# Weight chunks requested from ScalarE's queue, and the PSUM banks of the prologue divided anew

## The chip, the cores and the metric

The kernel runs on one core of one Trainium2 chip. A core has five engines that run beside each other, each through its own instructions in program order: TensorE (PE in the profile; its weight loads are PEld), VectorE (DVE), ScalarE (ACT), GpSimd (POOL) and SyncE (SP), which here does nothing but issue transfers. Sixteen DMA engines move the data. The metric is the device time of one execution in microseconds; less is better.

## The reference

Eight batches of eight heads, 576 positions, head size 64, all in fp32. Two attentions are added: one over queries, keys and values averaged in groups of four positions, its result repeated four times, and one in which each position sees the positions less than four away. The heads are then joined to 512 channels, mixed along the sequence by a product of rank 32, and put through a feed-forward network (FFN) with 2048 hidden channels.

```
q_d, k_d, v_d = means over groups of 4 positions       # 144 positions
out_d    = softmax(q_d k_d^T / 8) v_d
out_up   = repeat(out_d, 4)
scores   = q k^T / 8 where |i - j| < 4, else -1e9
x        = out_up + softmax(scores) v                  # heads joined: (8, 576, 512)
u        = x + (x^T U V)^T                             # U: 576 x 32, V: 32 x 576
y        = u + relu(u w_ch1) w_ch2                     # 512 -> 2048 -> 512
```

## The kernel before

**Precision.** TensorE multiplies the large products in fp32r, a shortened fp32. To keep fp32 accuracy each operand is held as a high and a low half, and each product is made of three: high times high, high times low, low times high. So one FFN step, 128 hidden channels of one tile of positions, is 12 matmuls into the hidden bank (`ffn1`, L944) and 12 into the four accumulators (`ffn2`, L969). The first two batches make four tiles of 288 positions, the other six nine tiles of 384. Between the two products ScalarE makes the high half of the rectified hidden values (hH, L952) and VectorE the low half (hL, L953).

**Weights.** Each of the two weight matrices comes in 16 chunks of 128 x 512 values that lie in memory as eight-byte numbers. A chunk (wr) is transferred raw, 512 KB, into the place that its converted form will take, and `convert` turns it into fp32 and splits it: ScalarE takes the upper 16 bits (half, L349), VectorE shifts them into a PSUM bank as y (L352) and joins them with the middle bits (c, L354), ScalarE makes the high half (W, L360), GpSimd the low half (W, L364). The smaller matrices U and V go the same way. `load_w` requests a chunk on SyncE (L416). The list `done` holds the merge step of each chunk so far, and a request is ordered behind the merge of the fourth chunk before it.

**The prologue.** The four head pairs of batch 0 are worked in the early form (`early_global`, `local_blocks`, `early_mix`, `u_tail`): local scores into PSUM banks 0 and 1 (ps_b), pooled scores (ps_s), softmax, products with the values (ps_a, ps_ba), the mixing with U (ps_hu, L708 and L710) and with V (ps_u, L726), and last the two halves uH and uL of the FFN's input. The windows of the values (vw, L598) have one buffer for all pairs. In batch 0 the mixing of a pair uses banks 0 and 1 too, and the conversions take banks 2 and 3 in turn, until 12 chunks are ordered; from then on a conversion uses the second hidden bank, and the FFN's first 19 steps have the other hidden bank alone. The FFN's accumulators take all four banks 0 to 3 from the first `ffn2` step on. The attention of the later batches runs in another form, much of it on GpSimd, through scratch memory in DRAM, while the FFN goes on.

**The order.** The order of all instructions is worked out by a planner in the kernel's Python code (`Plan`). Each operation has an engine, an assumed duration, a priority, what it depends on, and perhaps an earliest time. `run` steps through assumed time, takes for each engine the ready operation of least priority number, and models transfers with one clock `t_dma` on which they follow each other. The resulting list fixes each engine's program; on the chip each engine works through its own in order and waits only for data and buffers. That a request is ordered behind an earlier merge is the planner's doing and is no wait on the chip.

## Time and profile before

| | us |
|---|---|
| time before, median of 3 runs | 1009.38 (1004.36 to 1010.22) |
| profiled execution, its own time | 1009.23 |
| profiled execution, span | 1007.4 |
| TensorE busy | 974.7 |
| GpSimd busy | 571.5 |
| VectorE busy | 445.1 |
| ScalarE busy | 383.1 |

All profile lines are from that one profiled execution; times in them are microseconds from the start of the span, and mean durations are nanoseconds where a line says so. The names of engines are those given above; SPq is the queue of SyncE, whose DMA-issuing instructions, as those of any engine, do not count as busy time. "L416" is a line of the kernel. "out<-in" names what an instruction writes and reads, "x6" how many were taken together. A bracket at the end of a line gives the time for which the engine stood idle before the instruction, and what ended that wait; "issue" stands where the profile shows nothing that it waited for. PEclk, the granted clock, is the share of TensorE's full clock that it was given.

### The profile page before, as it was taken

Reading aid. Unit: us, or ns where it says so; the run is one execution under the profiler, and the core shown is the slowest. Engines: PE = TensorE matmul, PEld = TensorE weight load, DVE = VectorE, ACT = ScalarE, POOL = GpSimd, SP = SyncE. Lnnn points to the kernel's source line nnn. Section 1 sums busy time; section 2 is a strip of 40 time slices with the busy share of each in tenths; the row PEclk is TensorE's granted clock in tenths of the full one; section 3 lists DMA queues with packets and bytes.
Section 4 is the critical chain, followed back from the end, with each engine's and each line's share of the span. In section 5 each row is a group of like instructions: output and inputs, shape, how many; then the busy total and the mean of one; then the engine's idle time right before and its main releaser. Section 6 shows DMA issues by size and latency. Waiting matters only on the chain.

```text
span 1007.4 us, 24554 instructions
## 1 busy us (share of the span) xinstructions
PE 974.7 (97%) x9668; PEld 952.4 (95%) x9668; DVE 445.1 (44%) x852; ACT 383.1 (38%) x1191; POOL 571.5 (57%) x636
## 2 busy tenths in 40 slices
PE   6879999899999999999999999999999999999998
PEld 4769999898999999999999999999999999999998
DVE  5576855545544544544645445265351222211211
ACT  4676754443444443434545344444321222111110
POOL 6675997967858857857867766676650112300100
PEclk9789999999999999999999999999999999999999
DMA  9578876656546657455656366466330121000000
GB/s 275 160 268 239 211 173 143 156 129 152 138 111 161 161 127 149 129 127 139 158 136 146 80 162 148 98 164 146 82 94 1 21 59 25 32 1 1 32 1 32
DMA packets 221243, 120.06 MB, mean 119 GB/s; under 512 B 174580, under 2 KB 197448, under 8 KB 221128
## 3 DMA queue, kind: packets, MB, share of 16 engines
q1 hardware_dynamic: 221128, 118.50, 46.7%
q8 instruction: 76, 1.25, 0.5%
q14 instruction: 39, 0.32, 0.1%
HBM read 87.59 MB, written 30.86 MB: 118 GB/s over the span
## 4 chain that ended last, share of the span: by engine, by line
PE 80%; POOL 5%; DMA 4%; issue 2%; DVE 1%; ACT 1%; SPq 1%; POOLq 0%; DVEq 0%; ACTq 0%
PE acc L969 36%; PE ps_h L944 36%; PE ps_a L575 2%; PE ps_b L756 2%; PE ps_hu L919 2%; POOL W L364 2%; DMA ul<-up_s 1%; PE ps_t L562 1%; POOL Pt L840 1%; PE ps_b L769 1%; DMA vr<-in_v 1%; DMA wr<-in_W 1%; PE ps_u L726 1%; POOL gh L439 1%; POOL vr L533 0%
## 5 line engine op out<-in xcount | busy, mean ns | idle before, releaser
L969 PE MATMUL acc<-hH,W 128*128 128x384 f32 (+1 forms) x1664 | 443.8, 328 | 0.0
L944 PE MATMUL ps_h<-uH,W 128*128 128x384 f32 (+1 forms) x1376 | 359.1, 323 | 4.3 <-DVE hL L953 3.9
L969 PEld LDWEIGHTS acc<-hH,W 128*128 128x128 f32 x1664 | 297.6, 188 | 1.2
L969 PE MATMUL acc<-hL,W 128*128 128x384 f32 (+1 forms) x832 | 268.8, 323 | 0.0
L840 POOL TENSOR_TENSOR Pt<-vl,ms 128x896 f32<-128x896 f32 (+1 forms) x140 | 239.9, 1793 | 37.8 <-DMA vl<-in_vp 18.9
L944 PEld LDWEIGHTS ps_h<-uH,W 128*128 128x128 f32 x1376 | 245.5, 189 | 5.8 <-DVE hL L953 5.0
L953 DVE SCALAR_TENSOR_TENSOR hL<-ps_h,hH 128x384 fp32r<-128x384 f32 (+1 forms) x208 | 108.9, 524 | 314.9 <-ACT hH L952 314.4
L952 ACT ACTIVATE hH<-ps_h 128x384 fp32r<-128x384 f32 (+1 forms) x208 | 97.2, 467 | 329.7 <-PE ps_h L944 318.7
L944 PE MATMUL ps_h<-uL,W 128*128 128x384 f32 (+1 forms) x688 | 221.1, 321 | 0.5 <-POOL uL L735 0.5
L845 DVE TENSOR_REDUCE acc<-Pt 128x128 f32<-128x1024 f32 (+1 forms) x140 | 152.6, 1107 | 73.0 <-POOL Pt L840 40.7
L969 PEld LDWEIGHTS acc<-hL,W 128*128 128x128 f32 x832 | 156.6, 188 | 0.0
L944 PEld LDWEIGHTS ps_h<-uL,W 128*128 128x128 f32 x688 | 130.2, 189 | 0.8 <-POOL uL L735 0.7
L944 PE MATMUL ps_h<-u,W 128*128 128x384 f32 x432 | 99.6, 339 | 0.0
L834 ACT ACTIVATE Pt<-ul 128x128 f32<-128x128 f32 (+1 forms) x140 | 55.6, 432 | 95.7 <-DVE acc L845 68.6
L735 POOL TENSOR_TENSOR uL<-xT,uH 128x384 fp32r<-128x384 f32 (+2 forms) x52 | 41.1, 813 | 79.5 <-ACT uH L733 79.5
L979 POOL TENSOR_TENSOR o<-uH,uL 128x384 f32<-128x384 f32 (+1 forms) x43 | 39.1, 938 | 71.6 <-DMA out_t<-o 71.5
L944 PEld LDWEIGHTS ps_h<-u,W 128*128 128x128 f32 x432 | 77.4, 187 | 0.0
L911 POOL TENSOR_TENSOR xL<-xL,xH 116x640 fp32r<-116x640 f32 x28 | 43.9, 1567 | 56.9 <-ACT xH L910 56.6
L533 POOL TENSOR_TENSOR vr<-vr 72x256 f32<-72x256 f32 x56 | 41.4, 739 | 45.7 <-DMA vr<-in_v 36.1
L787 ACT ACTIVATE se<-ps_b 96x114 f32<-96x114 f32 x112 | 40.0, 357 | 47.9 <-PE ps_b L762 33.2
L364 POOL TENSOR_TENSOR W<-c,W 128x512 fp32r<-128x512 f32 x32 | 41.3, 1299 | 21.8 <-ACT W L360 21.8
L548 ACT ACTIVATE E<-ps_b,nb 72x144 f32<-72x144 f32 x112 | 40.7, 369 | 0.7
(131 smaller groups left out, 950.8 us busy)
## 6 DMA issues: line engine op xcount, KB each, us to landing
wr<-in_W SPq DMA_DIRECT2D x32, 511.8 KB
vl<-in_vp SPq DMA_DIRECT2D x56, 240.0 KB
vr<-in_v SPq DMA_DIRECT2D x64, 144.0 KB
gT<-in_kT SPq DMA_DIRECT2D x28, 291.0 KB
gq<-in_qT SPq DMA_DIRECT2D x28, 288.0 KB
up_s<-od SPq DMA_DIRECT2D x112, 72.0 KB
ul<-up_s SPq DMA_DIRECT2D x28, 288.0 KB
x_s<-acc SPq DMA_DIRECT2D x28, 288.0 KB
```

The source lines that it names most:

```text
L364: pool_tt(1.0 * n, lambda: nc.gpsimd.tensor_tensor(out=lo_out(), in0=ta()[l0:], in1=hi_out()[l0:].bitcast(F32), op=ALU.subtract), [t, *own ...
L533: pool_tt(256, lambda x=x: nc.gpsimd.tensor_tensor(out=x()[:, :, 0:2, :], in0=x()[:, :, 0:2, :], in1=x()[:, :, 2:4, :], op=ALU.add), [x], ...
L548: act(SD, lambda a=a, hh=hh, nb=nb: nc.scalar.activation(Es[hh]()[:, a, :], pooled_view(ps[hh])[:, a], AF.Exp, bias=nb()[:, a:a + 1], scal ...
L735: pool_tt(n, lambda uH=uH, uL=uL, uf=uf, us=us: nc.gpsimd.tensor_tensor(out=uL.ap(hp, us), in0=uf(), in1=uH.ap(hp, us).bitcast(F32), op=AL ...
L834: act(n * D, lambda n=n, ps=ps, Pt=Pt: nc.scalar.activation(Pt()[:, :n, :, 7], ul()[:, ps, :], AF.Copy), [ul], [(Pt, 1)], prio, 0.16)
L840: nc.gpsimd.tensor_tensor(out=Pt()[:, :n, :, 0:7].rearrange("p s d o -> p o s d"), in0=win, in1=at()[:, ps, :].rearrange("p s o -> p o s") ...
L845: dve(8.5 * n * D, lambda n=n, ps=ps, Pt=Pt: nc.vector.tensor_reduce(out=acc()[:, ps, :], in_=Pt()[:, :n], axis=AX.X, op=ALU.add), [(Pt, 0 ...
L911: pool_tt(640, lambda: nc.gpsimd.tensor_tensor(out=xL(), in0=xL().bitcast(F32), in1=xH().bitcast(F32), op=ALU.subtract), [xL, xH], [xL], prio)
L944: nc.tensor.matmul(ps()[:, :tn], W1[fc]()[:, w, dc, :], u.ap(dc), start=(n == 0), stop=(n == 3 * NDC - 1))
L952: last_h[i] = act(tn, lambda: nc.scalar.activation(hH()[:, :tn], ps()[:, :tn], AF.Relu), [ps], [hH], FIRST, 0.05)
L953: dve(tn, lambda: nc.vector.scalar_tensor_tensor(hL()[:, :tn], ps()[:, :tn], 0.0, hH()[:, :tn].bitcast(F32), op0=ALU.max, op1=ALU.subtract ...
L969: nc.tensor.matmul(ac[e]()[:, :tn], W2[fc]()[:, w, es], hx()[:, :tn], start=(fc == 0 and n == 0), stop=(fc == NFC - 1 and n == 2))
```

## The change

The raw chunks are requested by ScalarE, in its own instruction order and on its own transfer queue, instead of by SyncE. In the planner, a request is now an operation of ScalarE of 0.35 us with a transfer of 1.3 us behind it and an earliest time that rises by one microsecond per chunk from 12 us on; and each issuing engine has its own transfer clock, so that the two queues are taken to move data beside each other. The list `done` holds the step that makes the high half, instead of the merge. Up to the twelfth chunk every conversion uses bank 3; the mixing of batch 0 uses banks 2 and 1 where it used 0 and 1. No product, no conversion and no byte transferred is added or left out.

```diff
--- before.py
+++ after.py
@@ -103,7 +103,7 @@
             sharers.setdefault(k[:2], []).append(k)
         ready = [[] for _ in range(5)]
         pend = [[] for _ in range(5)]
-        t_eng, t_dma = [0.0] * 5, 0.0
+        t_eng, t_dma = [0.0] * 5, [0.0] * 5
         seq = {o: i for i, o in enumerate(self.ops)}
         got = set()
 
@@ -177,8 +177,7 @@
             t_eng[e] = end
             order.append((s, i, o))
             if o.move:
-                t_dma = max(t_dma, s + 1.1, end + 0.6 - 0.5 * o.move) + o.move
-                end = t_dma
+                end = t_dma[e] = max(t_dma[e], s + 1.1, end + 0.6 - 0.5 * o.move) + o.move
             done = end + o.lat
             for x in o.succ:
                 if done > x.ready:
@@ -227,6 +226,7 @@
     pw = lambda prio: PW0 if prio < 10 else PWx
     W1P = 30
     WD = 4
+    WAT, WAS = 12, 1
     HOLD = 1.5
     LEAD = 10.5
     NA = 12
@@ -307,7 +307,6 @@
     Upool = early_pool.tile([128, 2, 2 * R], F32, name="Upool")
     Ublk = early_pool.tile([128, NS, 2 * R], F32, name="Ublk")
     kept = {}
-    count = {"y": 0}
 
     def ring(shape, name, n=2, eng=None):
         if name not in kept:
@@ -339,8 +338,7 @@
         if own_bank:
             y = buf(ps_h, [128, CN], I32, "y_h", "h1:" + name, 1)
         else:
-            count["y"] += 1
-            y = buf(ps_acc, [128, CN], I32, "y_a", f"acc{2 + count['y'] % 2}:{name}", 1)
+            y = buf(ps_acc, [128, CN], I32, "y_a", f"acc3:{name}", 1)
         yi = lambda: y()[:pp, :n]
         ti = lambda: t()[:pp, :n]
         ta = lambda: ti().bitcast(F32).rearrange("p (a n) -> p a n", a=a)
@@ -355,9 +353,9 @@
             ti(), mid(), 13, yi(), op0=ALU.logical_shift_right, op1=ALU.bitwise_or), [raw, y], [t], prio)
         big = not isinstance(wkey, str)
         own = lambda k: [wkey + k] if isinstance(wkey, str) else [(wkey, k)]
-        if not isinstance(wkey, str):
+        act(n, lambda: nc.scalar.activation(hi_out(), ta(), AF.Copy, scale=1.0 if big else 256.0), [t], own("H"), prio)
+        if big:
             done.append(plan.ops[-1])
-        act(n, lambda: nc.scalar.activation(hi_out(), ta(), AF.Copy, scale=1.0 if big else 256.0), [t], own("H"), prio)
         if lo_out is None:
             return
         if big:
@@ -413,8 +411,8 @@
     def load_w(w, src, hi, lo, a, prio, dprio):
         weights.append(w)
         raw = buf(wts, [128, 2 * CN], I32, "wr", w.tag + ":raw")
-        dma(lambda: nc.sync.dma_start(out=raw().bitcast(U16)[:, :4 * CN - 1], in_=src), [], [raw], dprio, 525,
-            after=done[len(done) - WD:len(done) - WD + 1] if len(done) >= WD else ())
+        op(ACT, 0.35, lambda: nc.scalar.dma_start(out=raw().bitcast(U16)[:, :4 * CN - 1], in_=src), [], [raw], dprio,
+           done[len(done) - WD:len(done) - WD + 1] if len(done) >= WD else (), 1.3, 2.4, WAT + WAS * len(done))
         convert(raw, 128, CN, hi, lo, a, w, "c" + w.tag[1], prio, len(done) >= NA)
 
     def load_w1(f, prio):
@@ -678,7 +676,7 @@
         rd = [(x, g) for g in range(2)] + [(od, g) for g in range(2)]
         up = lambda a: od()[:, a].rearrange("p h d -> p (h d)")
         flat = lambda n: x()[:, n].rearrange("p h d -> p (h d)")
-        bank = lambda name, n: psum(ps_m, name, "m:x", 2) if b else psum(ps_acc, name, f"acc{n}:x", 1)
+        bank = lambda name, n: psum(ps_m, name, "m:x", 2) if b else psum(ps_acc, name, f"acc{2 - n}:x", 1)
         xT = buf(xts, [128, S], F32, "xT", bufs=HP)
         oT = buf(early_pool, [128, SD], F32, "oT", None, 1)
         q4 = 4 * 128
```

## The prediction

> **What bounds the kernel now.** I read the page first, then the engines' busy time by stretches of the run, then the issuing queue of SyncE and its waits, and last single rows of TensorE, VectorE and ScalarE where TensorE stood still.
>
> ```profile
> span 1007.4 us, 24554 instructions
> ...
> PE 974.7 (97%) x9668; PEld 952.4 (95%) x9668; DVE 445.1 (44%) x852; ACT 383.1 (38%) x1191; POOL 571.5 (57%) x636
> ```
>
> TensorE is the bound. It is idle for 1007.4 - 974.7 = 32.7 us, and nothing in this change takes a matmul away. So the change can save idle time and time at a reduced clock, nothing else. Where that time lies is in the stretches (columns: stretch, its length, busy time and count of PE, PEld, DVE, ACT, POOL, then granted clock, DMA share, GB/s).
>
> ```profile
> 0.00:64.20 64.20, 47.46 (x869) 39.35 (x870) 39.55 (x98) 39.67 (x126) 39.39 (x56) 0.89 0.72 225
> 64.20:125.00 60.80, 55.98 (x689) 53.54 (x688) 43.63 (x80) 42.28 (x107) 48.76 (x53) 0.97 0.84 240
> 125.00:196.00 71.00, 70.06 (x847) 68.78 (x845) 38.34 (x78) 35.33 (x122) 59.96 (x66) 1.00 0.65 149
> 196.00:206.00 10.00, 7.13 (x53) 6.75 (x54) 7.72 (x14) 3.45 (x12) 9.80 (x11) 0.83 0.73 198
> ```
>
> Length less PE time: 16.7 us idle up to the first FFN product (64.2 us), 4.8 in the stretch in which the other weight chunks arrive, 0.9 after it, 2.9 around 200 us. The rest of the run, 801 us, holds 32.7 - 25.3 = 7.4. Only the first 206 us are within reach.
>
> ```profile
> 15.00:20.00 5.00, 5.00 (x171) 4.19 (x171) 3.90 (x8) 2.98 (x8) 3.61 (x5) 1.00 1.07 342
> ...
> 40.00:45.00 5.00, 5.00 (x29) 4.81 (x30) 3.26 (x9) 1.76 (x5) 2.04 (x3) 0.50 0.42 167
> ...
> 64.20:75.00 10.80, 7.60 (x42) 6.92 (x41) 7.85 (x14) 7.10 (x14) 10.29 (x13) 0.84 0.86 279
> ```
>
> Early the DMA engines are full (share 1.07) and TensorE works without a gap; at 40 us it works without a gap at half clock while the DMA is at 0.42. Why the DMA has room there is in SyncE's queue.
>
> ```profile
> 48.79 0.79 SPq L598 DMA_DIRECT2D vw<-in_vw  x2
> 49.63 2.93 SPq L416 DMA_DIRECT2D wr<-in_W  x6
> ```
>
> ```profile
> SPq L598 <- PE ps_ba L667: 17.5, 2, 8.9
> ...
> SPq L416 <- DMA wr<-in_W: 3.0, 2, 1.5
> ```
>
> The load of the value windows vw has one buffer and waits for the last reader of the pair before (L667), 17.5 us in two waits. The six weight requests behind the second one wait for nothing of their own: they stand in line. That is what the change takes away.
>
> **The change part by part.**
>
> *The requests leave SyncE.* What one costs an issuing queue (count, shortest, median and longest ns), for those after 64.2 us:
>
> ```profile
> L416 SPq DMA_DIRECT2D wr<-in_W x17: 355/433/1696, 66.1 to 115.5; - x17
> ```
>
> There are 32 chunks, 16 of each weight matrix. SyncE gets back 32 x 0.433 = 13.9 us, 17 x 0.433 = 7.4 of them after 64.2 us, and no chunk stands behind vw any more. Pooled keys, queries and values move up in SyncE's queue. What late chunks cost shows in three places.
>
> *First, the end of the prologue.* Six chunks are requested at 49.6 us and converted while the last head pair is mixed:
>
> ```profile
> 56.74 0.73 PE L510 MATMUL ps_a<-vs_e,E_e 128*72 128x64 f32 x8 [0.31 <-ACT E_e L503]
> 58.23 0.34 PE L689 MATMUL ps_c<-ident_sb,od_e 72*128 72x72 f32 x2 [0.75 <-DVE od_e L513]
> 59.60 2.39 PE L708 MATMUL ps_hu<-ob,Ublk 128*64 128x128 f32 x10 [0.82 <-DVE xT L699]
> 63.80 0.54 PE L726 MATMUL ps_u<-Vst,stk 128*128 128x288 f32 x2 [0.95 <-DVE stk L714]
> ...
> 51.38 1.31 PE L708 MATMUL ps_hu<-ob,Ublk 128*64 128x128 f32 x10
> ```
>
> ```profile
> 57.29 0.69 DVE L352 TENSOR_SCALAR y_a<-half 128x512 int32<-128x512 int16 x1
> 57.89 0.28 DVE L513 TENSOR_TENSOR od_e<-ps_a,ri 72x128 f32<-72x128 f32 x1
> 58.09 0.67 DVE L354 SCALAR_TENSOR_TENSOR c<-wr,y_a 128x512 int32<-128x512 int32 x1
> ```
>
> ps_a ends at 56.74 + 0.73 = 57.47, and its eviction od_e starts at 57.89, behind a conversion: 0.4 us of the path. After these gaps L708 runs 2.39 us instead of 1.31 for the same work one pair earlier: 1.1 us to the slower clock. I count 0.4 and half of the 1.1: **0.9 us**. The ends are 0 and all four gaps with the clock, 0.31 + 0.75 + 0.82 + 0.95 + 1.1 = 3.9.
>
> *Second, after the first product.*
>
> ```profile
> 67.05 0.29 PE L944 MATMUL ps_h<-uH,W 128*128 128x288 f32 x1
> 69.67 0.56 PE L944 MATMUL ps_h<-uH,W 128*128 128x288 f32 x1 [2.33 <-DVE hL L953]
> ```
>
> ```profile
> 66.92 0.67 ACT L349 ACTIVATE half<-wr 128x512 f16<-128x512 bf16 x1
> 67.70 0.63 ACT L360 ACTIVATE W<-c 128x512 fp32r<-128x512 f32 x1
> 68.24 0.39 ACT L952 ACTIVATE hH<-ps_h 128x288 fp32r<-128x288 f32 x1
> ```
>
> The product ends at 67.34; its eviction waits behind two conversion steps until 68.24: 0.9 us. The stretch of 10.8 us at a mean clock of 0.84 also loses 1.7 us of clock. I count 0.9 and half of 1.7: **1.7 us**. Ends: 0, and the whole idle time with the clock, 10.8 - 7.6 + 1.7 = 4.9.
>
> *Third, batch 1.* TensorE reaches the second batch's tiles at about 196 us before their last mixing is ready:
>
> ```profile
> 196.09 0.52 PE L919 MATMUL ps_hu<-xH,Ust 116*64 116x128 f32 x5 [0.89 <-ACT xH L910]
> 197.72 0.51 PE L919 MATMUL ps_hu<-xL,Ust 116*64 116x128 f32 x5 [1.11 <-POOL xL L911]
> 199.90 0.82 PE L726 MATMUL ps_u<-Vst,stk 128*128 128x288 f32 x2 [1.67 <-DVE stk L924]
> ```
>
> That is 3.67 us, and 1.7 of clock (0.83 over 10 us): 5.4. GpSimd prepares that mixing, and in these stretches its chunk step (L364) took:
>
> ```profile
> 0.00:64.20 64.20, 12.72 (x10) 0.89 0.72 225
> 64.20:125.00 60.80, 27.32 (x21) 0.97 0.84 240
> ```
>
> 27.32 / 21 = 1.30 us a chunk. Up to 64.2 us ScalarE, VectorE and GpSimd were each idle some 24 us. A chunk costs ScalarE 0.67 + 0.63 + 0.43 for its request, VectorE 0.69 + 0.67, GpSimd 1.30, so six more fit there (10.4, 8.2 and 7.8 us), 16 instead of 10. Then GpSimd has 7.8 us less after 64 us, and SyncE 7.4 less; the wait is 3.67. The attention of batch 1 starts when the prologue ends, so both sides of this wait move together and the relief is not eaten up by the earlier start. I count two thirds: **3.6 us**; ends 0 and 5.4.
>
> *What ScalarE pays.* The trace shows no request on ScalarE, so the price is bounded by SyncE's rows: 13.9 us in all, against 24.5 us idle before 64.2 us and 18.5 in the next stretch. Only a request straight ahead of an operation that someone waits for costs. Queued behind it are softmax steps, the copies et and ob, and later the evictions hH, for which VectorE's hL and then TensorE wait. I take four such meetings, **1.7 us**; ends 0 and 13.9. A gain is excluded, since ScalarE issues nothing today.
>
> *Edits with a cost of nothing.* Ordering a request by the end of the chunk's high half instead of its merge (the list done) shifts an order by one ScalarE step, 0.63 us, hidden by four chunks in flight. One conversion bank instead of two: VectorE writes y and reads it back one after the other (57.29, then 58.09, the next y at 58.73), so the second bank was never used at once; without that cover the pair of steps, 1.36 us, would bound each of 12 chunks, far under the time in which they arrive. Mixing on bank 2 leaves bank 0 to the local scores, but these take banks 0 and 1 together and bank 1 still serves mixing: 0, at best a shift of TensorE's order while it is busy anyway. The planner's separate transfer clocks change only the order; they enter the rivals.
>
> *Sum.* -0.9 - 1.7 - 3.6 + 1.7 = -4.5 us. The profiled execution took 1009.2 us (1.8 outside its span), 0.2 under the median of 1009.38, so I put **1005 us**, with 999 to 1009 for this case.
>
> **The rivals.**
>
> *B, all stalls go.* With enough chunks ready TensorE never pauses long enough to lose its clock: 3.9 + 4.9 + 5.4 - 1.7 = 12.5 us, **997 us**; if the half-clock stretch from 40 us went too, 2.5 more. For it: each gap listed is followed by slow matmuls. Against it: TensorE also slowed at 40 us, behind a gap for which the profile shows no releaser ("issue"):
>
> ```profile
> 35.23 0.38 PE L667 MATMUL ps_ba<-vw,et 38*32 38x64 f32 x18 [2.67 <-issue]
> ```
>
> *C, nothing moves.* TensorE's order and the vw buffer set the prologue, the earlier chunks only take their share of a DMA that is full at 15 us, and the gain pays for ScalarE's requests: **1009 us**. For it: TensorE is busy 47.5 of 64.2 us, and the 17.5 us wait for L667 stays, since vw stays on SyncE. The Trainium skill, "DMA: Bandwidth & Descriptors", section "Issuing engines are not separate DMA queues", speaks for this case: transfers run on the same 16 engines whoever issues them, and a second issuer saves only issue time. The trace agrees in the first 30 us (share 1.07 on one queue); it does not at 40 us (share 0.42), where what was missing was the request.
>
> *D, slower: ScalarE is held by its requests.* On SyncE a request took up to 1.70 us and two of them waited 1.5 us each for an earlier transfer; and a chunk once kept the chain of waits for 8 us:
>
> ```profile
> 105.77 8.07 DMA wr<-in_W
> ```
>
> The planner now lets the two queues move data side by side, so it will place conversions before their chunk has landed, in a queue that works strictly in order. If each of the 17 late requests holds ScalarE for 1.5 us, that is 25.5 us against 18.5 - 7.4 = 11.1 us to spare: 14 us into the evictions, less the 0.9 of the prologue, **1022 us**. It decides once a request with its landing holds ScalarE more than 11.1 / 17 = 0.65 us beyond its issue. Against it: the second stretch will hold fewer requests if the prologue takes more.
>
> **How the numbers follow.** The forecast 0.42, B 0.22, C 0.16, D 0.20. A measurement of this kernel can tell about 1% (10 us) from no change. Faster by over 1%, under 999.3: B and the edge of the forecast, 0.27. Slower, over 1019.5: most of D, 0.16. Within: 0.57. The range from 993 to 1018 takes in the forecast, C, most of B and the light end of D; heavy D and B with the early clock are left out.
>
> **What would show it.** Right: no weight request behind vw on SyncE; 14 or more L364 steps before the first product, and that product before 62 us; hH within 0.3 us of its product; no wait over 1 us for mixing near 196 us; SyncE's L598 wait unchanged. Wrong: the first product not earlier (C); ScalarE idle for chunk landings, or TensorE waiting for hL in many steps up to 125 us (D); new gaps of TensorE with no releaser, as at 35 us, which no step here foresees. A reordering after 206 us that opens or closes waits there would also break the sum, since I put it at 0.

## The result, and the profile after

The changed kernel takes 1020.37 us (median; 1019.66 to 1025.29) against 1007.07 us for the kernel before on the same chip (1004.36 to 1010.22). The ratio is 1.014, with a 95% interval from 1.0106 to 1.0173: **slower by 1.4%**, where 0.4% faster was forecast. The profiled execution took 1020.45 us. In its line numbers everything behind the conversion stands two lower than before (L414 is the request, L347, L350, L352, L356 and L362 the five steps of a conversion, L942 and L967 the FFN products, L950 and L951 hH and hL).

The page first: the span, and the two queues in its part on DMA queues (queue, packets, MB, share of 16 engines).

```profile
span 1018.7 us, 24541 instructions
...
PE 976.4 (96%) x9668; PEld 953.7 (94%) x9668; DVE 446.4 (44%) x852; ACT 384.4 (38%) x1191; POOL 571.6 (56%) x636
...
q1 hardware_dynamic: 216520, 101.73, 41.0%
q10 hardware_dynamic: 4608, 16.77, 5.2%
```

All 32 chunks (16.77 MB) go through a queue of their own. The next rows are TensorE's timeline: the first FFN product before, and then, after the change, the first product and every gap of over 1 us up to the end of the conversions.

```profile
64.17 0.30 PE L944 MATMUL ps_h<-uH,W 128*128 128x288 f32 x1
```

```profile
58.02 0.30 PE L942 MATMUL ps_h<-uH,W 128*128 128x288 f32 x1
63.09 0.60 PE L942 MATMUL ps_h<-uH,W 128*128 128x288 f32 x1 [2.44 <-DVE hL L951]
67.96 0.45 PE L767 MATMUL ps_b<-smk,smq 64*32 64x144 f32 x12 [1.63 <-POOL smk L439]
86.05 0.40 PE L942 MATMUL ps_h<-uH,W 128*128 128x288 f32 x1 [3.01 <-DVE hL L951]
107.16 0.61 PE L942 MATMUL ps_h<-uH,W 128*128 128x288 f32 x1 [4.58 <-DVE hL L951]
127.83 0.40 PE L942 MATMUL ps_h<-uH,W 128*128 128x288 f32 x1 [1.49 <-DVE hL L951]
133.00 0.53 PE L967 MATMUL acc<-hH,W 128*128 128x288 f32 x2 [3.04 <-POOL W L362]
```

The first product starts at 58.02 us, 6.1 us earlier than before (64.17). From there to the end of the span it takes 1018.7 - 58.02 = 960.7 us, where it took 1007.4 - 64.17 = 943.2: 17.5 us are lost behind it, and 6.1 won ahead of it. I call the start of the first product the *product time*, and the time from there to the end the *rest*. By the trace's matmul records, TensorE stands still 23.2 us of the rest instead of 12.5 (+10.6), and its matmuls take 934.0 us instead of 927.3 (+6.7), since more of them run at half clock. The 400th FFN matmul after the first comes 92.2 us behind it instead of 70.6. Of the 23.2 us of standing still, 17.9 lie before 150 us, and 5.0 of the 12.5 in the kernel before. So the loss is made while weights are still being converted.

The 6.1 us won ahead of the product are mostly not a shorter wait. The columns of the next row, of the changed kernel, are those of the stretches in the prediction:

```profile
0.00:58.00 58.00, 42.39 (x868) 34.86 (x869) 36.81 (x93) 37.19 (x121) 36.92 (x54) 1.00 0.74 218
```

For the same matmuls TensorE needed 47.46 of 64.2 us before, at a mean clock of 0.89. So 5.1 us of the 6.1 are matmul time at a higher clock, and its idle time fell only from 16.7 to 15.6 us.

The stretches from 80 to 140 us by engines, before (first fence) and after (second):

```profile
80.00:100.00 20.00, 19.63 (x248) 19.05 (x247) 13.31 (x26) 14.29 (x38) 11.27 (x14) 1.00 0.80 229
100.00:120.00 20.00, 18.75 (x150) 18.03 (x148) 17.30 (x30) 14.72 (x40) 19.84 (x19) 1.00 0.88 228
120.00:140.00 20.00, 19.86 (x255) 19.37 (x255) 12.40 (x25) 11.47 (x36) 18.84 (x20) 1.00 0.63 139
```

```profile
80.00:100.00 20.00, 16.79 (x206) 16.20 (x189) 10.66 (x24) 13.07 (x38) 12.50 (x16) 0.91 0.81 242
100.00:120.00 20.00, 15.42 (x200) 14.70 (x198) 12.19 (x21) 10.09 (x26) 14.56 (x11) 0.83 0.62 175
120.00:140.00 20.00, 15.06 (x196) 13.80 (x196) 13.57 (x25) 11.01 (x30) 15.72 (x19) 0.91 0.87 221
```

TensorE falls from 58.2 to 47.3 of 60 us, and its clock below 1. But no other engine is fuller over the three stretches: VectorE, ScalarE and GpSimd do less as well (36.4, 34.2 and 42.8 us, from 43.0, 40.5 and 49.9). They wait. For what, the waits between 56 and 140 us say (engine and line, what it waited for, us in all, times, longest). Before:

```profile
PE ps_h L944 <- DVE hL L953: 3.9, 4, 2.3
...
POOL vr L533 <- DMA vr<-in_v: 1.5, 3, 1.1
```

After:

```profile
POOL vr L531 <- DMA vr<-in_v: 17.1, 5, 7.0
...
PE ps_h L942 <- DVE hL L951: 12.5, 7, 4.6
DVE lmx L811 <- DMA sc<-s_s: 11.1, 2, 6.2
...
ACT half L347 <- DMA vl<-in_vp: 4.6, 1, 4.6
```

GpSimd stands at vr, the values that it pools, and VectorE at lmx, the maximum over the local scores sc of a late pair, each for a load that SyncE issued. On the timelines of VectorE, GpSimd and ScalarE three such waits look like this:

```profile
105.14 0.22 DVE L811 TENSOR_REDUCE lmx<-sc 128x9 f32<-128x63 f32 x1 [6.18 <-DMA sc<-s_s]
```

```profile
131.00 0.72 POOL L531 TENSOR_TENSOR vr<-vr 72x256 f32<-72x256 f32 x1 [4.20 <-DMA vr<-in_v]
131.68 2.52 POOL L362 TENSOR_TENSOR W<-c,W 128x512 fp32r<-128x512 f32 x2
```

```profile
131.12 0.34 ACTq L414 DMA_DIRECT2D wr<-in_W  x1
131.56 0.67 ACT L347 ACTIVATE half<-wr 128x512 f16<-128x512 bf16 x1 [4.59 <-DMA vl<-in_vp]
```

The first holds every hL behind it, and TensorE's gap of 4.58 us at 107.16 follows; the gap of 3.01 us at 86.05 has a wait of lmx of the same kind ahead of it. The second holds GpSimd's chunk steps, and TensorE's gap of 3.04 us at 133.00 follows: the low half that it needs is the first of the two L362 steps, whose high half ScalarE had finished at 126.68. The third is of another kind. A conversion step (half) does not read vl. What waited was the request ahead of it. No gap of TensorE of over 1 us comes from this hold: the conversions that it delayed are of the next two chunks. The three gaps that do go back to waits for SyncE's loads, 3.01 + 4.58 + 3.04, make 10.6 us, as much as the idle time that the rest gained in all; smaller gaps came and went beside them.

How far the conversions are, in ScalarE's first step of each (L349 before, L347 after; busy time and count, clock, DMA):

```profile
80.00:100.00 20.00, 5.11 (x8) 1.00 0.80 229
100.00:120.00 20.00, 5.02 (x8) 1.00 0.88 228
120.00:140.00 20.00, 0.67 (x1) 1.00 0.63 139
```

```profile
80.00:100.00 20.00, 4.01 (x6) 0.91 0.81 242
100.00:120.00 20.00, 3.02 (x5) 0.83 0.62 175
120.00:140.00 20.00, 3.71 (x6) 0.91 0.87 221
```

A step that crosses a border counts in both stretches, and the four conversions of U and V are counted too. Before, the last conversion starts soon after 120 us; after, one is under way then and five have still to start. Up to 80 us both kernels have started 20. The written order says the same: on ScalarE 14, 16, 22 and 28 conversions stand ahead of the 1st, 4th, 8th and 12th step of the hidden layer in the kernel before, and 11, 14, 21 and 26 in the changed one. I call these four numbers the *stock*; each hidden step uses two chunks, one of each matrix.

### The profile page after: what moved, and what is told of

It reads as the page before. It is cut to its first block, busy times and chain, and to the rows that moved or that the text cites. A ratio compares the mean times of both kernels' runs of the same rounds, so it can differ in the third digit from the quotient of the medians.

```text
span 1018.7 us, 24541 instructions
## 1 busy us (share of the span) xinstructions
PE 976.4 (96%) x9668; PEld 953.7 (94%) x9668; DVE 446.4 (44%) x852; ACT 384.4 (38%) x1191; POOL 571.6 (56%) x636
## 3 DMA queue, kind: packets, MB, share of 16 engines
q10 hardware_dynamic: 4608, 16.77, 5.2%
## 4 chain that ended last, share of the span: by engine, by line
PE 74%; POOL 7%; DMA 3%; issue 2%; ACT 2%; SPq 1%; DVE 1%; ACTq 0%; POOLq 0%; DVEq 0%
PE acc L967 33%; PE ps_h L942 33%; POOL Pt L838 3%; PE ps_a L573 2%; PE ps_b L754 2%; DMA vr<-in_v 2%; PE ps_hu L917 1%; PE ps_b L767 1%; PE ps_t L560 1%; DMA s_s<-se 1%; SPq L793 1%; POOL o L977 1%; PE ps_u L724 1%; POOL uL L733 1%; POOL gh L437 1%
## 5 line engine op out<-in xcount | busy, mean ns | idle before, releaser
L967 PE MATMUL acc<-hH,W 128*128 128x384 f32 (+1 forms) x1664 | 445.1, 329 | 3.2 <-POOL W L362 3.2
L942 PE MATMUL ps_h<-uH,W 128*128 128x384 f32 (+1 forms) x1376 | 362.4, 325 | 13.1 <-DVE hL L951 12.5
L967 PEld LDWEIGHTS acc<-hH,W 128*128 128x128 f32 x1664 | 299.4, 189 | 4.7 <-POOL W L362 3.7
L967 PE MATMUL acc<-hL,W 128*128 128x384 f32 (+1 forms) x832 | 269.9, 324 | 0.0
L942 PEld LDWEIGHTS ps_h<-uH,W 128*128 128x128 f32 x1376 | 247.4, 191 | 15.2 <-DVE hL L951 14.0
L838 POOL TENSOR_TENSOR Pt<-vl,ms 128x896 f32<-128x896 f32 (+1 forms) x140 | 240.3, 1797 | 28.1 <-DVE acc L843 15.6
L951 DVE SCALAR_TENSOR_TENSOR hL<-ps_h,hH 128x384 fp32r<-128x384 f32 (+1 forms) x208 | 109.0, 524 | 326.6 <-ACT hH L950 325.7
L942 PE MATMUL ps_h<-uL,W 128*128 128x384 f32 (+1 forms) x688 | 222.6, 323 | 1.4 <-POOL uL L733 1.4
L950 ACT ACTIVATE hH<-ps_h 128x384 fp32r<-128x384 f32 (+1 forms) x208 | 97.1, 467 | 314.1 <-PE ps_h L942 302.9
L967 PEld LDWEIGHTS acc<-hL,W 128*128 128x128 f32 x832 | 157.6, 189 | 0.0
L942 PEld LDWEIGHTS ps_h<-uL,W 128*128 128x128 f32 x688 | 131.4, 191 | 1.9 <-POOL uL L733 1.9
L942 PE MATMUL ps_h<-u,W 128*128 128x384 f32 x432 | 99.7, 339 | 0.0
L942 PEld LDWEIGHTS ps_h<-u,W 128*128 128x128 f32 x432 | 77.5, 188 | 0.0
L531 POOL TENSOR_TENSOR vr<-vr 72x256 f32<-72x256 f32 x56 | 41.5, 741 | 63.3 <-DMA vr<-in_v 63.3
L362 POOL TENSOR_TENSOR W<-c,W 128x512 fp32r<-128x512 f32 x32 | 41.1, 1291 | 11.1 <-ACT W L356 11.1
```

The costliest lines, as they stand in the source:

```text
L362: pool_tt(1.0 * n, lambda: nc.gpsimd.tensor_tensor(out=lo_out(), in0=ta()[l0:], in1=hi_out()[l0:].bitcast(F32), op=ALU.subtract), [t, *own ...
L531: pool_tt(256, lambda x=x: nc.gpsimd.tensor_tensor(out=x()[:, :, 0:2, :], in0=x()[:, :, 0:2, :], in1=x()[:, :, 2:4, :], op=ALU.add), [x], ...
L838: nc.gpsimd.tensor_tensor(out=Pt()[:, :n, :, 0:7].rearrange("p s d o -> p o s d"), in0=win, in1=at()[:, ps, :].rearrange("p s o -> p o s") ...
L942: nc.tensor.matmul(ps()[:, :tn], W1[fc]()[:, w, dc, :], u.ap(dc), start=(n == 0), stop=(n == 3 * NDC - 1))
L950: last_h[i] = act(tn, lambda: nc.scalar.activation(hH()[:, :tn], ps()[:, :tn], AF.Relu), [ps], [hH], FIRST, 0.05)
L951: dve(tn, lambda: nc.vector.scalar_tensor_tensor(hL()[:, :tn], ps()[:, :tn], 0.0, hH()[:, :tn].bitcast(F32), op0=ALU.max, op1=ALU.subtract ...
```

## The experiments

Three theories, and what each predicts:

- **S, the stock.** The product comes early because conversions were put behind it; TensorE then runs short of converted weights.
- **P, the place.** The planner keeps a separate clock for the transfers of each issuing engine. It takes SyncE's loads as free of the chunks, expects them too soon, and writes VectorE's and GpSimd's steps ahead of the landing.
- **R, the requests.** A request on ScalarE waits for an older transfer, and all of ScalarE's work stands behind it. 25 of the 32 requests in the changed kernel carry a wait on one of eight completion counters, which the transfers of both queues share.

All ratios are to the kernel before, in runs on the same chip beside it. Its median there lay between 1006.6 and 1013.3 us, so microseconds of different groups aren't compared. Product time, rest and wait are read from one profiled execution each, and executions of one kernel lay up to 12.5 us apart (e18): a few microseconds in these columns can be chance. The ratios rest on 4 to 10 executions of each changed kernel and 4 to 22 of the kernel before. "Wait" is GpSimd's for landings between 56 and 140 us.

| kernel | order written with | requests on | ratio (95% interval) | product time | rest | stock | wait |
|---|---|---|---|---|---|---|---|
| before | one clock | SyncE | 1 | 64.2 | 943.2 | 14, 16, 22, 28 | 1.5 |
| after | two clocks | ScalarE | 1.014 (1.0106 to 1.0173) | 58.0 | 960.7 | 11, 14, 21, 26 | 19.3 |
| e1_one_clock | one clock, new request | ScalarE | 1.0165 (1.013 to 1.020) | 67.0 | 955.3 | 11, 15, 20, 23 | 1.2 |
| e2_after_order_sync | as after | SyncE | 1.0074 (1.0046 to 1.0101) | 59.3 | 954.7 | as after | 14.0 |
| e3_before_order_act | as before | ScalarE | 1.0014 (0.9985 to 1.0043) | 63.5 | 944.2 | as before | 2.0 |
| e4_sc_late | two clocks, sc later | ScalarE | 1.011 (1.0081 to 1.0139) | 58.2 | 957.2 | 11, 14, 21, 27 | 15.4 |
| e5_banks_only | one clock | SyncE | 0.9955 (0.9929 to 0.9981) | 61.5 | 947.9 | as before | 0 |
| e6_split_order | as after | 13 on ScalarE | 1.0093 (1.0063 to 1.0123) | 64.0 | 963.0 | as after | 17.2 |
| e7_split_planned | two clocks, 13 chunks | 13 on ScalarE | 1.0049 (1.0019 to 1.0078) | 60.9 | 952.9 | 11, 14, 20, 25 | 7.6 |
| e8_wd8 | two clocks | ScalarE | 1.0131 (1.0072 to 1.0191) | 61.4 | 957.7 | 12, 15, 22, 28 | 9.9 |
| e9_first15_act | as e5 | 15 on ScalarE | 0.9984 (0.9955 to 1.0012) | 62.9 | 949.9 | as before | 1.9 |
| e10_no_earliest | two clocks | ScalarE | 1.0122 (1.0069 to 1.0176) | 69.1 | 955.4 | 13, 17, 23, 29 | 13.1 |
| e11_low_stock | one clock, late requests | SyncE | 1.0106 (1.0056 to 1.0157) | 57.3 | 966.7 | 10, 12, 19, 24 | 0.2 |
| e12_no_earliest_sync | as e10 | SyncE | 1.0137 (1.0088 to 1.0185) | 63.3 | 963.2 | as e10 | 12.8 |
| e13_stock_and_sc | two clocks, sc later | ScalarE | 1.0099 (1.0069 to 1.0128) | 69.8 | 954.1 | 13, 17, 24, 29 | 13.9 |
| e14_stock_and_sc_sync | as e13 | SyncE | 1.0135 (1.009 to 1.018) | 66.3 | 955.2 | as e13 | 11.6 |
| e15_more_stock | two clocks, sc later | ScalarE | 1.0082 (1.0055 to 1.0108) | 66.6 | 948.7 | 15, 18, 24, 29 | 18.4 |
| e16_one_clock_full_stock | one clock, new request | ScalarE | 1.0117 (1.0086 to 1.0148) | 72.5 | 947.5 | 15, 17, 23, 29 | 2.7 |
| e17_one_clock_done_new | one clock, new request | ScalarE | 1.013 (1.0086 to 1.0173) | 68.9 | 951.7 | 16, 18, 24, 29 | 8.3 |
| e18_old_order_all_act | as e5 | ScalarE | 1.0025 (0.9988 to 1.0062) | 62.2 | 947.2 | as before | 0.4 |

### Order and issuer taken apart

e1 gives the changed kernel the planner's one clock back:

```diff
-        t_eng, t_dma = [0.0] * 5, [0.0] * 5
+        t_eng, t_dma = [0.0] * 5, 0.0
...
-                end = t_dma[e] = max(t_dma[e], s + 1.1, end + 0.6 - 0.5 * o.move) + o.move
+                t_dma = max(t_dma, s + 1.1, end + 0.6 - 0.5 * o.move) + o.move
+                end = t_dma
```

> The changed kernel with one line of the planner put back: all transfers follow each other on one assumed clock, whichever queue issues them. Requests stay on ScalarE, banks and the list done stay as changed. In the changed kernel VectorE stood 5.0 and 6.2 us before the local maximum lmx (waiting for the load sc), and TensorE then 3.0 and 4.6 us for hL. Theory P (the split clock makes the planner place work that needs SyncE's loads too early in VectorE's order; there lmx comes behind 4 and 8 of the hL steps where it came behind 7 and 13 before): with one clock the order has lmx behind 7 and 12 again, both waits go, and the earlier first product (58 instead of 64 us) is kept: 998 to 1006 us. Theory R (requests hold ScalarE, as my rival D said): the holds stay, 1015 to 1022 us.

e2 keeps the changed kernel's order and lets SyncE issue:

```diff
-        op(ACT, 0.35, lambda: nc.scalar.dma_start(out=raw()...
+        op(ACT, 0.35, lambda: nc.sync.dma_start(out=raw()...
```

> The changed kernel's order of all instructions, but each chunk request stands in SyncE's queue at the place where it stood in ScalarE's. Theory P: VectorE's order is the same, so the two waits for sc and TensorE's 3.0 and 4.6 us stay, and chunks are late behind vw again: 1018 to 1030 us. Theory R: nothing holds ScalarE any more, so it comes back to 1003 to 1010 us.

e3 is the kernel before with `nc.scalar.dma_start` in place of `nc.sync.dma_start` and no other edit:

> The order of the kernel before, but each chunk request is issued by ScalarE at the place that it has in that order. Theory P: VectorE's order is that of before, no wait of 5 us for sc; chunks no longer stand behind vw, so the first product comes 1 to 4 us earlier: 1000 to 1008 us. Theory R: 32 requests in ScalarE's queue with their waits hold the evictions: 1015 to 1025 us.

e4 is the changed kernel, with the planner told that the load sc of the first late pairs lands 9 us later:

```diff
-            [(s_s, hh) for hh in range(2)], [sc], prio, 315, lat=0.8)
+            [(s_s, hh) for hh in range(2)], [sc], prio, 315, lat=9.8 if prio < 55 else 0.8)
```

> The changed kernel; the planner only assumes 9 us more for the load sc of the first two late head pairs, which puts lmx behind 6 and 13 of the hL steps instead of 4 and 8. Requests stay on ScalarE. Theory P: TensorE's 3.0 and 4.6 us and the half-clock time behind them (3.4 and 6.8 us, worth 1.7 and 3.4) go: 1020 - 12.7 = 1008, 1006 to 1012 us. Theory R: 1018 to 1022 us, unchanged.

P as first put, two clocks as the whole cause, fell: e1 has no wait of lmx left and stays 1.65% slower, with a late product and the lowest stock of the first four. R as the whole cause fell too: ScalarE's requests in the old order change nothing that can be measured (e3), and the new order on SyncE (e2) keeps half of the loss, between what P and R foresaw. In e4 lmx stands about where it stood in the kernel before (behind 6 and 13 hL steps; 7 and 13 there, 4 and 8 in the changed kernel) and its waits are gone, but other holds come to light. On ScalarE's timeline of e4:

```profile
88.08 0.34 ACTq L414 DMA_DIRECT2D wr<-in_W  x1
88.46 0.30 ACT L543 ACTIVATE nb<-mx 72x2 f32<-72x2 f32 x2 [3.28 <-DMA vr<-in_v]
...
117.05 0.33 ACTq L414 DMA_DIRECT2D wr<-in_W  x1
117.48 0.66 ACT L347 ACTIVATE half<-wr 128x512 f16<-128x512 bf16 x1 [3.72 <-DMA s_s<-se]
```

Neither step reads what it is said to wait for. As at 131.12 in the changed kernel, the releaser is a landing for which the request ahead waited. Here a gap of TensorE follows the second hold at once, for the hidden values' high half hH stands behind it:

```profile
118.98 0.40 PE L942 MATMUL ps_h<-uH,W 128*128 128x288 f32 x1 [3.31 <-DVE hL L951]
```

R is real, then, but only a part.

### The other edits alone

e5 has the bank edits in the kernel before, and nothing else:

```diff
-            count["y"] += 1
-            y = buf(ps_acc, [128, CN], I32, "y_a", f"acc{2 + count['y'] % 2}:{name}", 1)
+            y = buf(ps_acc, [128, CN], I32, "y_a", f"acc3:{name}", 1)
...
-        bank = lambda name, n: psum(ps_m, name, "m:x", 2) if b else psum(ps_acc, name, f"acc{n}:x", 1)
+        bank = lambda name, n: psum(ps_m, name, "m:x", 2) if b else psum(ps_acc, name, f"acc{2 - n}:x", 1)
```

> The kernel before with the bank edits alone (conversion halves in acc3 only, the two mixing banks swapped); SyncE still issues every chunk and the planner is the old one. If the bank edits cost nothing, as the prediction had it: 1004 to 1010 us, first FFN product about 60 us after the first matmul. If one conversion bank holds the prologue up (each half waits for the conversion before it): the prologue 2 us or more longer and 1010 to 1014 us. A gain below 1002 us would mean that early mixing was held by the bank it shared.

They gain 0.45%, and the interval leaves 1 out: of all kernels of this study, this one alone is measurably faster than the kernel before. Its product time is 2.7 us less. Its rest came out 4.7 us longer in the one profiled execution, so where the gain lies isn't shown.

e6 and e7 leave only the first 13 requests to ScalarE. In e6 SyncE issues the other 19 from the same places; in e7 they are planned as SyncE's transfers. The edit of e6:

```diff
+        issuer = nc.scalar if len(done) < 13 else nc.sync
-        op(ACT, 0.35, lambda: nc.scalar.dma_start(out=raw()...
+        op(ACT, 0.35, lambda: issuer.dma_start(out=raw()...
```

> The changed kernel's own order of work, but only its first 13 chunks (those ahead of the first FFN product) are issued by ScalarE; the other 19 are issued by SyncE from the same places in the order. Theory R (a request holds ScalarE while it waits for an older transfer to land): prologue as in the changed kernel, span after the first product near the 951 us of the run in which SyncE issued all of them, so 1011 to 1015 us. Theory P (the order costs, whoever issues): also some 8 us above the kernel before, 1013 to 1016 us. If it is neither, and it is the first 13 requests on ScalarE that cost: 1018 us or more.

> The changed kernel, planned anew with its first 13 chunks as ScalarE's operations and the other 19 as SyncE's transfers on SyncE's clock of the planner, as before the change. The maximum lmx stands behind 5 and 9 hL steps here (4 and 8 in the changed kernel, 7 and 13 in the kernel before). Theory R alone: ScalarE is free after the first product, so the late loss goes: prologue 55 us after the first matmul and 942 to 945 us after the product, 999 to 1003 us. Theory P: lmx still stands some hL steps too early and waits 1 to 4 us for the load sc twice, so 1004 to 1012 us.

e6 comes out at e2's ratio within the intervals, as R and P both foresaw, so it does not tell them apart; its interval overlaps the changed kernel's too. In its one profile the product is 6 us later than in the changed kernel, in the same order and with the same issuer up to there: the clock was 0.82 up to the product, and 1.00 in the changed kernel. e7 is the best of the orders planned with two clocks, and still 0.5% slower than the kernel before: with no lmx wait, a wait of 7.6 us and a low stock.

In e8 a request is ordered behind the conversion eight chunks back (WD = 8 instead of 4):

> The changed kernel with each chunk's request ordered behind the conversion eight chunks back in place of four. The prediction's missing step was that more chunks would be asked for before the first product. If more requests come before it (16 or more of 32 in place of 13) and theory R holds: fewer requests late, and 4 to 8 us of the 17 us lost after the product come back, 1010 to 1016 us. If the number of requests before the product stays at 13 or so, since the planner's due times and not the distance of four set it: no change, 1018 to 1022 us.

17 requests come before the product instead of 13 and the rest is 3.0 us shorter, but the product is 3.3 us later. Moving chunks ahead of the product is an exchange here, not a gain.

### The stock by itself

e9 (e5, with the first 15 chunks issued by ScalarE) looked for a kernel that beats e5:

> The kernel before with the bank edits, in its old order, and only the requests of the first 15 chunks (those ahead of the first FFN product) issued by ScalarE from the places where SyncE had them; the other 17 stay with SyncE. Theory R: no request stands between ScalarE's steps after the product, and none of the first 15 is queued behind SyncE's load vw any more, so the prologue is 2 us shorter than in the run of the bank edits and the rest the same: ratio to the kernel before 0.992 to 0.996. If issuing on ScalarE costs wherever it is done: 0.998 to 1.003.

It doesn't, at 0.9984. e10 drops the earliest time from the changed kernel (the first edit below), and e12 is its twin on SyncE. e11 puts a low stock into e5 (the second):

```diff
-           done[...] if len(done) >= WD else (), 1.3, 2.4, WAT + WAS * len(done))
+           done[...] if len(done) >= WD else (), 1.3, 2.4, 0)
```

```diff
         dma(lambda: nc.sync.dma_start(out=raw()...
+        plan.ops[-1].ready = max(plan.ops[-1].ready, 16 + 2 * len(done))
```

> The changed kernel without the rule that chunk n may not be asked for before 12 + n us. 13 chunk conversions stand ahead of the first hidden step on ScalarE and 29 ahead of the twelfth (changed kernel: 11 and 26; kernel before: 14 and 28). Theory S (the early first product is paid for with conversions that are left for later, and TensorE runs short of weights until the last of them, near 130 us): first product 2 to 4 us later than in the changed kernel, 8 us or more less lost after it, 1012 to 1016 us. Theory P (lmx standing too early) and theory R (requests hold ScalarE) see no change here, since lmx stands behind 5 and 7 hL steps and ScalarE still issues all: 1018 to 1022 us.

> The kernel before with the bank edits, SyncE issuing every chunk and the planner's one clock, but with an earliest time of 16 + 2n us for chunk n: 10 chunk conversions stand ahead of the first hidden step and 24 ahead of the twelfth (14 and 28 without it), while lmx keeps its late places (behind 7 and 12 hL steps). Theory S: the loss comes back without any request on ScalarE and without lmx waiting: first product 2 to 6 us earlier, 8 to 14 us more after it, ratio to the kernel before 1.003 to 1.010. Theories P and R: nothing that they name is in it, so as the bank edits alone, 0.993 to 0.998.

> The order of the run without an earliest time, with every request issued by SyncE from the same places. What it is below that run is what the requests on ScalarE cost in this order. Theory R: 4 to 8 us less than that run. Theory S with no share of R: the same within 2 us. If S and R together are all of it, it comes within 0.3% of the kernel before.

e11 is the run made for S alone. Its waits between 56 and 140 us:

```profile
PE ps_h L944 <- DVE hL L953: 8.5, 6, 2.5
...
POOL vr L533 <- DMA vr<-in_v: 0.2, 1, 0.2
```

and its first conversion steps, counted as above:

```profile
80.00:100.00 20.00, 4.98 (x8) 1.00 0.96 267
...
120.00:140.00 20.00, 2.71 (x4) 1.00 0.57 127
```

No request on ScalarE, no GpSimd wait, lmx in its old place: and the product is 4.2 us earlier than in e5, four conversions are left after 120 us (none in e5), and the whole is 1.5% slower than e5 (1.0106 against 0.9955). The 400th FFN matmul comes 7.7 us later behind the first than in e5, the 1000th 10.4. The remaining 8 us of the longer rest (966.7 against 947.9) arise after 240 us, with new gaps of 1.68 us (310 us) and 2.52 (322 us): the plan differs there too, and S doesn't explain that part. Nor does the trace bear out S as it was put. The earlier product is matmul time again, 41.0 us against 45.0 in e5, with 16.3 and 16.5 us of idle time ahead of it. And behind it TensorE waits for hL (8.5 us), hardly for converted weights (0.5 us, GpSimd's L363). So e11 shows that an order with fewer conversions ahead can lose without P and R; that the stock does it, and how, isn't shown by this run alone.

e10 went against S as I had put it: a stock as good as before's brought nothing (1.0122). GpSimd still waited 13.1 us, lmx 9.7, and the product came at 69.1. Its twin e12 is no faster, so R is not what holds these two:

```profile
ACT half L347 <- DMA wr<-in_W: 15.4, 8, 4.5
...
DVE lmx L811 <- DMA sc<-s_s: 9.2, 2, 8.9
POOL vr L531 <- DMA vr<-in_v: 8.9, 4, 4.3
```

With SyncE issuing, ScalarE waits for the chunk instead of at the request: 15.4 us. The last column of the table now shows P in a wider form than lmx. In every order planned with two clocks GpSimd waits 7.6 to 19.3 us for landings; in every order planned with one, 0 to 2.0 up to this point.

### Both causes taken away

e13 has e10's and e4's edits together, e14 is the same on SyncE, and e15 also orders the request by the merge again, as the kernel before does:

> The changed kernel without the earliest time of a request and with the planner told that the load sc of the first two late pairs lands 9 us later: 13 conversions ahead of the first hidden step and 29 ahead of the twelfth, lmx behind 7 and 11 hL steps (kernel before: 14, 28, 7 and 13). ScalarE issues all requests. If S and P together are the loss: no wait of lmx over 2 us, and the ratio to the kernel before 0.994 to 1.002. If R is the larger part: 1.007 to 1.013, with TensorE's long waits for hL under requests that hold ScalarE.

> The same order with every request issued by SyncE. S and P the whole loss: within 0.3% of its twin with ScalarE. R: 4 to 8 us under it.

> As the first of these, with the request of a chunk again ordered behind the shift-and-or of the chunk four back instead of behind its high half: 15 conversions ahead of the first hidden step, 18 ahead of the fourth, 24 ahead of the eighth and 29 ahead of the twelfth, lmx behind 8 and 13 hL steps. Theory S: TensorE waits less after the product than in the kernel before (under 12 us in all), and if the first product comes no more than 3 us later, the ratio is 0.990 to 0.998. If R decides: 1.004 to 1.012 here too.

lmx no longer waits (0 to 0.5 us), but GpSimd does (11.6 to 18.4 us), and the ratios stay at 1.008 to 1.0135. Telling the planner about one load isn't enough. SyncE issuing is again no better. But in e15, with the longest of these waits of GpSimd, the rest is 948.7 us: the wait by itself has no fixed price. Its longest gap of TensorE, 5.57 us at 75.06, is R's: hH stands behind a request that goes out when the load gq has landed.

e16 has one clock, no earliest time, the chunk priced at 1.82 us, and the request ordered by the merge; e17 is the same with the changed kernel's order of the request:

```diff
-           done[...] if len(done) >= WD else (), 1.3, 2.4, WAT + WAS * len(done))
+           done[...] if len(done) >= WD else (), 1.3, 1.82, 0)
```

> The changed kernel with one clock for all transfers in the planner, no earliest time, the chunk priced at 1.82 us of that clock (2.4 in the changed kernel) and the next request ordered behind the shift-and-or of the chunk four back: 15 conversions ahead of the first hidden step, 17, 23 and 29 ahead of the fourth, eighth and twelfth, lmx behind 7 and 13 hL steps. ScalarE issues all requests. S and P the whole loss: GpSimd waits under 3 us for landings between 56 and 140 us, TensorE is idle 11 to 15 us after the product, and the ratio to the kernel before is 0.994 to 1.002. If issuing on ScalarE has a price of its own: 1.005 to 1.012.

> As its twin, but with the next request ordered behind the high half, as in the changed kernel: 16, 18, 24 and 29 conversions ahead, lmx behind 5 and 12 hL steps. S and P in the wide form: the same as its twin within 0.4%. If the place of lmx is what decides in P: a wait of lmx of 2 us or more and 0.3 to 0.8% above its twin.

After the product e16 does what S and P say: TensorE stands still 15.8 us, and the rest is 947.5, 13.2 us less than in the changed kernel and 4.3 over the kernel before, with ScalarE issuing every chunk. A hold of R is its longest gap too: 4.40 us at 79.75, with hH behind a request that goes out at 78.41, when gq has landed. e17 is half way (951.7), with 8.3 us of GpSimd's wait back though it was planned on one clock: the rule on clocks has an exception. e16's waits between 56 and 140 us:

```profile
DVE lmx L812 <- DMA sc<-s_s: 2.5, 1, 2.5
...
POOL vr L532 <- DMA vr<-in_v: 0.9, 1, 0.9
```

But the ratio stays 1.0117, because the product now comes at 72.5 us. On TensorE's timeline of e16:

```profile
10.23 1.07 PE L611 MATMUL ps_b<-kd,qt 64*32 64x38 f32 x72 [4.67 <-DMA kd<-in_kT]
21.90 1.24 PE L469 MATMUL ps_s<-smk,smq 64*72 64x144 f32 x8 [10.60 <-POOL smk L440]
```

Without the earliest time, chunk requests crowd into the first 12 us (four in e16, none in the changed kernel), and the attention's own first inputs come late: up to the product TensorE stands still 28.7 us, and 15.6 in the changed kernel. That rule bought something, then: it shields the opening, and pays with the stock. It isn't all, for e1 keeps the rule and its product comes at 67.0.

e18 is the last: the old order, the bank edits, and all 32 requests on ScalarE.

> The kernel before in its old order with both of the things that the change does on the chip: all 32 requests issued by ScalarE, and the banks as changed. If the loss lies in the order alone: ratio to the kernel before 0.994 to 1.002, first product 57 to 60 us after the first matmul and 939 to 947 us after it. If requests on ScalarE have a price of their own that the run without the bank edits did not show: 1.005 to 1.012.

At 1.0025 it can't be told from the kernel before. All that the change does on the chip, without the order that its planner writes, costs at most 0.6% against the kernel before.

### What the runs add up to

Four runs have the same banks and differ in order and issuer: old order and SyncE 0.9955 (e5), old order and ScalarE 1.0025 (e18), new order and SyncE 1.0074 (e2), new order and ScalarE 1.014 (the change). So the order costs 1.2% with either issuer, ScalarE as the issuer 0.7% in either order, and the banks gain 0.45%: -0.45 + 0.7 + 1.2 = 1.45, the measured 1.4. **The larger part is shown: it is the order.** What in the order costs is only in part shown. For P stand the three gaps of the changed kernel, 10.6 us, that go back to loads on SyncE. For S stands the whole table: in every order whose stock begins with 13 or less the rest is 952.9 us or more, and with 14 or more it is 951.7 or less, whichever engine issues and however long GpSimd waits (e15). That is a correlation over single profiles, and S's own mechanism, a product made early by leaving out conversions and then a shortage of converted weights, isn't seen in the traces. The two don't add: orders with one of them cured (e1 for P; e10, e13 and e14 for S) still lose 1.0 to 1.65%, in part by their late products. How the 1.2% divides stays open, and so does which edit of the planner makes the order worse, as e1, with one clock, is no faster.

ScalarE's 0.7% is less sure. The intervals of both pairs are just apart, but without the bank edits it is 0.14% (e3), and the twins e10 with e12 and e13 with e14 have ScalarE 0.15 and 0.36% ahead. Its size stays open.

## Why the prediction was wrong, point by point

- **Where the time can be: right.** TensorE's work is unchanged, and everything moved within the first 214 us. Its own warning, an effect past 206 us, did not decide.
- **"Six more chunks fit there, 16 instead of 10": this step failed.** Only 13 requests and 8 GpSimd steps (L362) came before the product, fewer than before. I took idle engine time for an invitation. What sets the number is the planner, and its rules were in the diff: without "no chunk n before 12 + n us" there were 15 requests (e10), and with a request ordered eight chunks back instead of four 17 (e8). The first product was early although fewer conversions stood ahead of it, so it was not early by the path that I foresaw. The GpSimd time that I had counted as freed after 64 us was spent waiting.
- **The end of the prologue (0.9, at most 3.9): too small.** The product came 6.1 us earlier. TensorE's clock was 1.00 from 40 to 58 us, 0.84 before, and 5.1 of the 6.1 us are shorter matmul time; the forecast had left that clock to rival B's "if". That the number of this part went the right way is luck: why the clock held isn't shown, and in e6, with the same order up to the product, it didn't.
- **After the first product (1.7): failed.** The same wait for hL is there, 2.44 us at 63.09 against 2.33, and larger ones follow.
- **Batch 1 (3.6): failed.** In place of the three gaps around 196 us, 3.67 us, there are 1.04 + 0.63 + 0.84 = 2.5 near 211, so 1.2 us less. But the half clock behind them lasted longer, 6.8 us against 3.4, and costs 1.7 us more: nothing was gained.
- **What ScalarE pays (1.7 for four meetings): mis-sized.** One hold alone took 4.6 us, though no gap of TensorE came from it. I had bounded a request by the durations of SyncE's rows, up to 1.70 us; the wait ahead of it isn't in them. By the pairs of runs the price is about 7 us, and uncertain. That is within the 0 to 13.9 given.
- **Banks at nothing: off by 0.45%**, on the good side.
- **"The separate transfer clocks change only the order": the costliest sentence.** The order is what a planned kernel is. I gave it no term in the sum, and the new order, with everything in the planner that was changed, was worth 1.2%, about 12 us.
- **The rivals.** The sign was D's, and its sentence on the planner (conversions placed before their chunk has landed) named half of P. But D priced ScalarE's holds alone, 14 us; the greater loss sat in VectorE and GpSimd, in steps that have nothing to do with the weights. The Trainium skill, "DMA: Bandwidth & Descriptors", section "Issuing engines are not separate DMA queues", had been given to C: a second issuer saves only issue time. e18 and e3 agree with it, at 1.0025 and 1.0014 nothing was gained by the second queue. (The share of 1.07 that the prediction gives beside it is that of 15 to 20 us; over the first 30 us it is 0.95.) Of B only the "if" came: up to the first product the clock stayed at 1.00 from 40 us on, but TensorE paused more behind it, not less.
- **The signs.** Seen as said: the product before 62 us, SyncE's wait for vw unchanged (16.0 us in three waits), TensorE waiting for hL up to 125 us (D). Not seen: 14 or more GpSimd steps before the product; hH within 0.3 us of its product (the first came 1.0 us behind it, at 61.66); and one wait for mixing is still just over 1 us (1.04).

## What to carry to other kernels

Where a planner writes the order, a change to its cost model is a change to every engine's queue: compare the two written orders first (how many conversions stand ahead of each consumer, what stands in front of a load), and price that before any hardware effect. An earlier first product is no gain by itself. Read it together with the time from there to the end, and ask whether it came from shorter waits or from the clock. And if the planner keeps a clock for each queue, look for engines that wait for landings: here those waits were 7.6 to 19.3 us on GpSimd, and 0 to 2.7 (once 8.3) on one clock. One clock alone did not make a faster kernel (e1).

## What the runs showed of the hardware that was not expected

- A request on a compute engine can hold it far longer than it takes to issue: the issue took 0.33 us in the median (at most 1.33 in the changed kernel and 1.81 in e4), and the holds ahead of it 2.96 to 4.59 us. The landing it waited for belonged to other tensors (vl, vr, s_s) that SyncE had asked for.
- TensorE's clock fell again and again in the middle of a full run: 0.83 in the stretch from 100 to 120 us of the changed kernel, that is (1 - 0.83) x 20 / 0.5 = 6.8 us at half clock. The gaps of 2.44, 3.01, 4.58 and 3.04 us each went with a stretch at 0.50 (63.1 to 66.4, 87.0 to 90.3, 104.1 to 110.7 and 134.8 to 138.0 us); those of 1.63 and 1.49 us did not (1.00 from 66.6 to 86.8 and from 110.9 to 134.6). But the three gaps near 211, none over 1.04 us, did (213.3 to 220.0). In all, the rest held 23.9 us of half clock against 6.8 before. By the matmul times above that adds some 6.7 us to the 10.6 us of standing still.
